# A byte limit on the loads under way in the first blocks of an attention and softplus-FFN kernel

## The chip, the cores and the metric

The kernel runs on one core of a Trainium2 chip. Its time is the device time of one execution in microseconds (us); of several executions the median is given. A core has five engines that run side by side, each with its own queue of instructions in a fixed order: PE (TensorE, matmuls), DVE (VectorE), ACT (ScalarE), POOL (GpSimd) and SP (SyncE, which here only issues transfers). The transfers themselves are carried out by 16 DMA engines. Engines wait for each other, and for transfers, on semaphores.

## The reference

The input is `q`, `k`, `v` of shape (4, 8, 768, 64) in float32 and two weight matrices in float64, `w_in` (512 x 2048) and `w_out` (2048 x 512). First comes a linear attention with a decay per head, then a feed-forward layer with softplus:

```python
for t in range(S):                      # S = 768
    state = gamma * state + outer(k[:, :, t], v[:, :, t])
    y[:, :, t] = scale * (q[:, :, t] @ state)
x = y.transpose(0, 2, 1, 3).reshape(3072, 512)
h = x @ w_in
g = maximum(h, 0) + log1p(exp(-abs(h)))
out = g @ w_out
```

## The kernel before

**Tiles.** The 3072 tokens are cut into 6 blocks of 512, and each block into 4 units of 128 tokens. A unit of attention loads its `q`, `k` and `v` (`qn`, `kn`, `vn`: 768 KB for all 8 heads; `q` and `k` as two transfers of 128 KB, `v` as one of 256 KB), scales `q` and `v` by the decay (POOL, L444 and L440), turns `q` and `k` on PE (L466, L474), copies them to `kt` (ACT, L481 and L482), and makes scores, states and outputs by 64x64 matmuls. Its result `x` is held as a high and a low part. The feed-forward layer goes over 16 slices `f` of 128 hidden columns: `hp = x @ w_in[:, f]`, softplus on DVE and ACT (L671 to L674, with the high part `gh` by ACT and the low part `gl` by POOL), and `acc += g @ w_out[f]`. All products are made of three matmuls, from high and low parts.

**Weights.** Each slice needs two loads of 512 KB of float64 words (`raw`): one of `w_in` (L362) and one of `w_out` (L364). They are taken apart on ACT and DVE (L369, L373, L379, L384, L389), and stored as a high part (ACT, L392) and a low part (POOL, L393). This is done once, in the first blocks of work, beside the attention and the matmuls that use the first slices.

**What sets the order.** A planner in the kernel collects all operations with a cost, a due time and their dependencies, plays them through with a clock of its own, and puts them out by planned start. Loads are operations of the engine SP with `size / rate` as cost (the helper `DMA`), so the order in which SP issues transfers is fixed at build time. The orders are tied down for every engine in `emit`.

**What SP waits for.** All transfers that matter here are issued by SP, one after the other; while one waits, all behind it wait. A load waits for the engines that last used its buffer. Beside that, landings are told by eight semaphores (DMAHW0 to DMAHW7) used in turn, each load taking the next one, so that a load waits for the landing of the one eight places before it.

**The first rows of SP.** In the order of SP, rows 1 to 13 load the attention units c00, c01 (half of the heads each) and c1; rows 14 and 15 load `w_in` of slices 0 and 1; rows 16 to 20 load the unit c2; rows 21 and 22 load `w_out` of slices 0 and 1; rows 23 to 27 load c3; rows 30 and 31 are `w_in` of slices 2 and 3, rows 32 and 35 `w_out` of slices 2 and 3. Rows 1 and 2 hold two loads each; every other row is one load. Rows 42, 46 and 48 are `w_in` of slices 4, 5 and 6, rows 45, 47 and 49 the `w_out` of these slices.

Of the kernel before, what the change touches and what calls it, by code (L numbers as in the profile page):

```python
# [30 lines left out]
PAIRED = 8  # L31
AFTER = 1000
FLIGHT = 3
VISITS = (1,3,6,9,11,14)
FILL = (8, 20, 15, 150)
EASY = 2
# [206 lines left out]
def decay_attention_then_softplus_ffn(ctx: ExitStack, tc: tile.TileContext, q, k, v, w_in, w_out, qtab, vtab, gtab, out):  # L243
# [14 lines left out]

    behind = mybir.DependencyInfo(mybir.DependencyClass.NoSync, mybir.DependencyReason.SCHED_ONLY)
    last = {}  # L260

    def emit(i):
        e = i.ins.engine
        if e in last:
            tc.add_manual_dep(i.ins, last[e], behind, reason="program order")
        last[e] = i.ins.name
        return i

    plan = Planner()
# [70 lines left out]
        return op  # L340

    def DMA(size, run, after=(), uses=(), at=None, rate=340.0):
        return plan.add("SP", size / rate, run, after, uses, at)

    mm = lambda o, l, r, start, stop: emit(nc.tensor.matmul(o, lhsT=l, rhs=r, start=start, stop=stop))  # L345


    wdone, pace = {}, []

    def convert_weights(f):  # L350
        n = ND * P
        fs = slice(f * P, (f + 1) * P)
        for nm in ("win", "wout"):
# [6 lines left out]
            def load(raw=raw, nm=nm):  # L360
                if nm == "win":
                    emit(nc.sync.dma_start(buf(raw).rearrange("p (c w) -> p c w", c=ND), w_in[:, fs].rearrange("(c p) w -> p c w", p=P)))  # L362
                else:
                    emit(nc.sync.dma_start(buf(raw), w_out[fs, :]))  # L364

            bits = lambda held: bank(held).bitcast(U32)
            free = [ys[u] for u in range(BORROW)] if f"{nm}{f}" in LATE else []
            ld = DMA(8 * P * n, load, free + [pace[-2 * FETCH]] if len(pace) >= 2 * FETCH else [], [raw])
            a = ACT(685, lambda word=word: emit(nc.scalar.activation(word(1).bitcast(F32), word(1).bitcast(F32), AF.Copy, scale=2.0**-112)), [ld], [raw])  # L369
            if nm == "wout" or f < EASY:  # L370
# [30 lines left out]
    def unit(p, first, G, when, paired):  # L401
# [27 lines left out]
        def fetch(size, run, held):  # L429
            loads.append(DMA(size, run, loads[-FLIGHT:-FLIGHT + 1] if paired else [], [held], when[0] - LOAD, 200.0))  # L430
            return loads[-1]
# [198 lines left out]
    def ffn_step(s, h, i, f, when, past_ops=()):  # L630
# [74 lines left out]
        for t in ts:  # L705
            acc, done = accs.pop((i, t))
            ob = hold_w(queue=False)
            if i == NB - 1:
                ob.among += ["win1", "win2"]
            if t % 2:  # L710
                o = ACT(scalar_time(DM), lambda acc=acc, ob=ob: emit(nc.scalar.copy(buf(ob), bank(acc))), [done[-1]], [acc, ob], when[1] + 3000)
            else:
                o = DVE(vector_time(DM), lambda acc=acc, ob=ob: emit(nc.vector.tensor_copy(buf(ob), bank(acc))), [done[-1]], [acc, ob], when[1] + 3000)
            r = slice(TURN[i * NT + t] * P, (TURN[i * NT + t] + 1) * P)
            DMA(4 * P * DM, lambda r=r, ob=ob: emit(nc.sync.dma_start(out[r, :], buf(ob))), [o], [ob], when[1] + 3000)
# [82 lines left out]
    for i, f in fs:  # L798
# [4 lines left out]
        if i < NB - 1:  # L803
# [3 lines left out]
            while m < min(target + EXTRA, NT * (i + 2), PAIRED):  # L807
                units((m, 0, 2, whens))
                m += 1
            if NT * (i + 1) >= PAIRED and f in VISITS:  # L810
                at = VISITS.index(f)
                if at % 3 == 0:
# [5 lines left out]
        ffn_step(None, None, i, f, (now - early * step, now + hidden_time + second_time + AFTER), past_ops)  # L818
        now += step + PACE

    ordered = plan.order()
    for op in ordered:
        op.run()


# [28 lines left out]
```

## Time and profile before

| | |
|---|---|
| runs | 755.79, 620.13, 622.18 us; median 622.18 us |
| profiled execution | 619.63 us, of which the span of instructions is 617.9 us |
| PE | 607.9 us busy, 98% of the span |
| PEld (weight loads) | 498.0 us, 81% |
| DVE, ACT, POOL | 241.2, 227.4, 239.9 us (37 to 39%) |
| data moved | 42.80 MB, mean 69 GB/s |
| granted TensorE clock | 1.0 throughout |

The span is what lies between the first and the last instruction; 1.7 us of the profiled execution lie outside it. Times in the trace count from the start of the span. "Idle before" is the time an engine stood still just before an instruction, with what ended the wait behind the arrow. A row of the list of DMA issues gives the kind, the number of loads, the size of one in KB and the microseconds from issue to landing; in a narrow window it is that of a single load.

### The profile page before, as it was taken

How to read it: one execution, taken by the hardware profiler on the slowest of the kernel's cores; microseconds unless marked ns; L12 is line 12 of the kernel's file. 1: busy time of each engine (PE TensorE's matmuls, PEld its weight loads, DVE VectorE, ACT ScalarE, POOL GpSimd, SP SyncE). 2: the span in 40 equal slices, each digit the busy share in tenths (PEclk: the TensorE clock that was granted, in tenths of full speed). 3: DMA queues.
4: the chain of work that ended last, by engine and by line, in shares of the span. 5: the costliest groups of instructions: out<-in, count | busy, mean ns of one | idle time of the engine just before them, and what ended most of it. 6: DMA issues, size and time to landing. Idle time of an engine off the chain costs nothing.

```text
span 617.9 us, 13254 instructions
## 1 busy us (share of the span) xinstructions
PE 607.9 (98%) x5635; PEld 498.0 (81%) x5635; DVE 241.2 (39%) x438; ACT 227.4 (37%) x407; POOL 239.9 (39%) x206
## 2 busy tenths in 40 slices
PE   8799999999999999999999999999999999999997
PEld 5688888888888878888888888888888888888886
DVE  4688776733323233322423332333323233322231
ACT  3768757641432234133134233143223313322221
POOL 3677768641342252153153143235225223222221
PEclk9999999999999999999999999999999999999999
DMA  7997566130120032040032031012103000100001
GB/s 187 267 282 221 187 210 184 57 103 2 35 54 16 2 86 86 1 87 17 3 86 86 1 82 25 1 45 76 53 2 86 1 1 1 69 1 1 1 0 68
DMA packets 90442, 42.80 MB, mean 69 GB/s; under 512 B 77072, under 2 KB 85264, under 8 KB 90384
## 3 DMA queue, kind: packets, MB, share of 16 engines
q1 hardware_dynamic: 89936, 41.95, 24.6%
q8 instruction: 44, 0.72, 0.5%
q14 instruction: 14, 0.11, 0.1%
q10 hardware_dynamic: 448, 0.01, 0.0%
HBM read 35.66 MB, written 6.29 MB: 68 GB/s over the span
## 4 chain that ended last, share of the span: by engine, by line
PE 95%; DMA 1%; SPq 1%; ACT 1%; DVE 1%; issue 0%; POOL 0%; ACTq 0%
PE hp L345 44%; PE acc L345 44%; PE a L345 4%; DMA raw<-in_moe_w_in_dram 1%; PE a L466 1%; PE a L474 1%; PE hp L466 1%; SPq L427 1%; DMA qn<-in_q_dram 0%; SPq L424 0%; DVE sp L673 0%; POOL win L393 0%; ACT gh L674 0%; ACT sp L672 0%; SPq L362 0%
## 5 line engine op out<-in xcount | busy, mean ns | idle before, releaser
L345 PE MATMUL hp<-x,win 128*128 128x512 f32 (+1 forms) x1176 | 278.0, 385 | 0.5 <-POOL win L393 0.5
L345 PEld LDWEIGHTS hp<-x,win 128*128 128x128 f32 x1176 | 217.4, 188 | 44.6 <-POOL win L393 0.7
L675 POOL TENSOR_TENSOR gl<-sp,gh 128x512 fp32r<-128x512 f32 x90 | 116.0, 1289 | 278.7 <-ACT gh L674 186.0
L345 PE MATMUL acc<-wout,gh 128*128 128x512 f32 x736 | 192.2, 396 | 0.5 <-DVE x L562 0.5
L345 PEld LDWEIGHTS acc<-wout,gh 128*128 128x128 f32 x736 | 134.9, 188 | 31.0 <-ACT gh L674 0.8
L671 DVE TENSOR_SCALAR sp<-hp 128x512 uint32<-128x512 uint32 x92 | 63.6, 691 | 243.5 <-PE hp L345 167.5
L672 ACT ACTIVATE sp<-sp 128x512 f32<-128x512 f32 x92 | 58.1, 632 | 261.1 <-DVE sp L671 261.0
L345 PE MATMUL acc<-wout,gl 128*128 128x512 f32 x368 | 104.8, 390 | 0.0
L673 DVE SCALAR_TENSOR_TENSOR sp<-hp,sp 128x512 f32<-128x512 f32 x92 | 63.5, 691 | 52.7 <-ACT sp L672 52.3
L345 PEld LDWEIGHTS acc<-wout,gl 128*128 128x128 f32 x368 | 69.0, 188 | 14.6
L674 ACT CAST gh<-sp 128x512 fp32r<-128x512 f32 x90 | 55.8, 620 | 60.0 <-DVE sp L673 59.9
L444 POOL TENSOR_TENSOR qn<-qn,tabs 128x512 f32<-128x512 f32 (+1 forms) x23 | 23.8, 1034 | 31.9 <-DMA qn<-in_q_dram 31.7
L596 POOL TENSOR_TENSOR x<-xs,x 128x512 fp32r<-128x512 f32 x20 | 25.6, 1295 | 12.6 <-ACT x L595 12.6
L440 POOL TENSOR_TENSOR vn<-vn,tabs 128x512 f32<-128x512 f32 (+1 forms) x24 | 24.2, 1010 | 8.2 <-DMA vn<-in_v_dram 8.0
L393 POOL TENSOR_TENSOR win<-w,win 128x512 fp32r<-128x512 f32 x16 | 20.6, 1293 | 8.5 <-ACT win L392 7.9
L369 ACT ACTIVATE raw<-raw 128x512 f32<-128x512 f32 x32 | 21.4, 676 | 6.8 <-DMA raw<-in_moe_w_in_dram 3.8
L393 POOL TENSOR_TENSOR wout<-w,wout 128x512 fp32r<-128x512 f32 x16 | 20.6, 1297 | 5.4 <-ACT wout L392 5.4
L384 DVE SCALAR_TENSOR_TENSOR a<-raw,a 128x512 uint32<-128x512 uint32 x28 | 19.2, 691 | 2.1 <-ACT a L373 1.7
L389 DVE SCALAR_TENSOR_TENSOR w<-raw,a 128x512 uint32<-128x512 uint32 x28 | 18.9, 683 | 1.6 <-POOL wout L393 0.5
L500 DVE TENSOR_TENSOR ah<-a,mask 128x256 uint32<-128x256 uint32 x27 | 10.3, 420 | 13.9 <-PE a L345 13.9
L592 DVE TENSOR_TENSOR xs<-a,xs 128x256 f32<-128x256 f32 (+1 forms) x24 | 8.8, 409 | 17.7 <-ACT xs L586 17.5
L595 ACT CAST x<-xs 128x512 fp32r<-128x512 f32 x20 | 12.4, 620 | 2.6 <-DVE xs L592 2.5
(138 smaller groups left out, 390.7 us busy)
## 6 DMA issues: line engine op xcount, KB each, us to landing
raw<-in_moe_w_in_dram SPq DMA_DIRECT2D x16, 512.0 KB, 6.3
raw<-in_moe_w_out_dram SPq DMA_DIRECT2D x16, 512.0 KB, 6.8
qn<-in_q_dram SPq DMA_DIRECT2D x44, 128.0 KB, 3.1
kn<-in_k_dram SPq DMA_DIRECT2D x44, 128.0 KB, 3.5
vn<-in_v_dram SPq DMA_DIRECT2D x22, 256.0 KB, 3.7
out_dram<-w SPq DMA_DIRECT2D x22, 256.0 KB, 2.2
out_dram<-win SPq DMA_DIRECT2D x2, 256.0 KB, 2.1
qn<-in_q_dram SPq DMA_DIRECT2D x4, 64.0 KB, 2.4
```

The source lines that it names most:

```text
L345: mm = lambda o, l, r, start, stop: emit(nc.tensor.matmul(o, lhsT=l, rhs=r, start=start, stop=stop))
L369: a = ACT(685, lambda word=word: emit(nc.scalar.activation(word(1).bitcast(F32), word(1).bitcast(F32), AF.Copy, scale=2.0**-112)), [ld], [ ...
L384: lambda word=word, wp=wp: emit(nc.vector.scalar_tensor_tensor(bits(wp), word(1), 0x80000000, bits(wp), op0=ALU.bitwise_and, op1=ALU.bitwi ...
L393: low_ = POOL(1300, lambda nm=nm, w=w: emit(nc.gpsimd.tensor_tensor(hl(nm, f)[:, 1], buf(w), hl(nm, f)[:, 0].bitcast(F32), op=ALU.subtract ...
L440: emit(engine.tensor_tensor(heads(held), heads(held), by, op=ALU.mult))
L444: emit(engine.tensor_tensor(all_, all_, by, op=ALU.mult))
L596: xl = POOL(2.53 * E * C, lambda: emit(nc.gpsimd.tensor_tensor(xo(1), buf(xs)[:, :E], xo(0).bitcast(F32), op=ALU.subtract)), [xh] + xdeps, ...
L671: a = DVE(vector_time(T), lambda: emit(nc.vector.tensor_scalar(U(spv()), U(bank(hp)), 0x80000000, None, op0=ALU.bitwise_or)), [lasts[-1]] ...
L672: b = ACT(640, lambda: emit(nc.scalar.activation(spv(), spv(), AF.Softplus)), [a], [sp])
L673: c = DVE(vector_time(T), lambda: emit(nc.vector.scalar_tensor_tensor(spv(), bank(hp), 0.0, spv(), op0=ALU.max, op1=ALU.add)), [b], [hp, sp])
L674: e = ACT(scalar_time(T, False), lambda: emit(nc.scalar.copy(buf(gh), spv())), [c], [sp, gh])
L675: g = POOL(1300, lambda: emit(nc.gpsimd.tensor_tensor(buf(gl), spv(), buf(gh).bitcast(F32), op=ALU.subtract)), [e], [sp, gh, gl])
```

## The change

Each SP operation now remembers its size. When the planned order is put out, each load adds up sizes backwards over the loads before it, beginning with its own. The load at which the sum passes 1,300,000 bytes is the one it must wait for: a wait on the landing of that load. Waits are added only where the planned start of the load lies before 60 us. The order on all engines is the same as before, row by row.

```diff
+UNDERWAY = 1.3e6
+SETTLED = 60000
...
     last = {}
+    issued = []
 
     def emit(i):
         e = i.ins.engine
         if e in last:
             tc.add_manual_dep(i.ins, last[e], behind, reason="program order")
         last[e] = i.ins.name
+        issued.append(i.ins)
         return i
...
     def DMA(size, run, after=(), uses=(), at=None, rate=340.0):
-        return plan.add("SP", size / rate, run, after, uses, at)
+        op = plan.add("SP", size / rate, run, after, uses, at)
+        op.size = size
+        return op
...
+    landed = mybir.DependencyInfo(mybir.DependencyClass.Sync, mybir.DependencyReason.DATA)
+    moved = []
     ordered = plan.order()
     for op in ordered:
         op.run()
+        if op.engine == "SP":
+            total = op.size
+            for size, instruction in reversed(moved):
+                total += size
+                if total > UNDERWAY:
+                    if op.start < SETTLED:
+                        tc.add_manual_dep(issued[-1], instruction.name, landed, reason="bytes under way")
+                    break
+            moved.append((op.size, issued[-1]))
```

What differs is what SP waits for. These are rows 14 to 22 of SP before (`raw` are weights, `qn`, `kn`, `vn` the inputs of unit c2):

```order
L362 DMA raw_190<-in_moe_w_in_dram 128x4x128 [waits DMAHW3_49]
L362 DMA raw_192<-in_moe_w_in_dram 128x4x128 [waits DMAHW4_49]
L427 DMA qn0_213<-in_q_dram 128x4x64 [waits DMAHW5_49,DVE_49,PE_49]
L427 DMA qn0_213<-in_q_dram 128x4x64 [waits DMAHW6_49]
L427 DMA kn0_230<-in_k_dram 128x4x64 [waits DMAHW7_49,DVE_49,PE_49]
L427 DMA kn0_230<-in_k_dram 128x4x64 [waits DMAHW0_49]
L424 DMA vn0_251<-in_v_dram 128x8x64 [waits DMAHW1_49,PE_49,Pool_49]
L364 DMA raw_260<-in_moe_w_out_dram 128x512 [waits DMAHW2_49]
L364 DMA raw_272<-in_moe_w_out_dram 128x512 [waits DMAHW3_49]
```

And the same rows now:

```order
L368 DMA raw_190<-in_moe_w_in_dram 128x4x128 [waits DMAHW6_49,DMAHW3_49]
L368 DMA raw_192<-in_moe_w_in_dram 128x4x128 [waits DMAHW4_49,DMAHW2_49]
L433 DMA qn0_213<-in_q_dram 128x4x64 [waits DMAHW5_49,DVE_49,PE_49]
L433 DMA qn0_213<-in_q_dram 128x4x64 [waits DMAHW3_49]
L433 DMA kn0_230<-in_k_dram 128x4x64 [waits DMAHW7_49,DVE_49,PE_49]
L433 DMA kn0_230<-in_k_dram 128x4x64 [waits DMAHW0_49]
L430 DMA vn0_251<-in_v_dram 128x8x64 [waits DMAHW1_49,DMAHW4_49,PE_49,Pool_49]
L370 DMA raw_260<-in_moe_w_out_dram 128x512 [waits DMAHW5_49]
L370 DMA raw_272<-in_moe_w_out_dram 128x512 [waits DMAHW1_49]
```

A row r uses the semaphore (r + 5) mod 8. Row 15 waited for row 7 (DMAHW4) and now also for the landing of row 13 (DMAHW2), the 256 KB of `v` just two places before it. Row 17 waits for row 14 (DMAHW3), row 20 for row 15 (DMAHW4), row 22 for row 20 (DMAHW1): two places back, where it was eight. Where a semaphore has gone from a row, an earlier row of SP already waits for the same landing or a later one.

Rows 30 to 35 before, two `w_in`, a `w_out`, two loads of `q`, a `w_out`:

```order
L362 DMA raw_403<-in_moe_w_in_dram 128x4x128 [waits DMAHW3_49]
L362 DMA raw_410<-in_moe_w_in_dram 128x4x128 [waits DMAHW4_49]
L364 DMA raw_488<-in_moe_w_out_dram 128x512 [waits DMAHW5_49]
L427 DMA qn1_507<-in_q_dram 128x4x64 [waits DMAHW6_49,PE_49,Pool_49]
L427 DMA qn1_507<-in_q_dram 128x4x64 [waits DMAHW7_49]
L364 DMA raw_519<-in_moe_w_out_dram 128x512 [waits DMAHW0_49]
```

And now:

```order
L368 DMA raw_403<-in_moe_w_in_dram 128x4x128 [waits DMAHW6_49]
L368 DMA raw_410<-in_moe_w_in_dram 128x4x128 [waits DMAHW4_49,DMAHW1_49]
L370 DMA raw_488<-in_moe_w_out_dram 128x512 [waits DMAHW5_49,DMAHW3_49]
L433 DMA qn1_507<-in_q_dram 128x4x64 [waits PE_49,Pool_49]
L433 DMA qn1_507<-in_q_dram 128x4x64 [waits DMAHW7_49,DMAHW4_49]
L370 DMA raw_519<-in_moe_w_out_dram 128x512 [waits DMAHW5_49,DMAHW0_49]
```

Row 32 now waits for row 30 (DMAHW3), and row 35 for row 32 (DMAHW5); row 35 had waited for row 27 (DMAHW0). The last row with an added wait is row 57, which waits for row 54.

## Prediction

> **What bounds the kernel now.** I read the page first, for who is busy when.
>
> ```profile
> PE 607.9 (98%) x5635; PEld 498.0 (81%) x5635; DVE 241.2 (39%) x438; ACT 227.4 (37%) x407; POOL 239.9 (39%) x206
> GB/s 187 267 282 221 187 210 184 57 103 2 35 54 16 2 86 86 1 87 17 3 86 86 1 82 25 1 45 76 53 2 86 1 1 1 69 1 1 1 0 68
> ```
>
> PE is busy 98% of the span, and the transfers are dense in the first seven of 40 slices alone (7 x 15.4 = 108 us). Next come the windows, split where PE's real matmuls begin and where it has no gaps any more.
>
> ```profile
> 0.00:20.40 20.40, 15.76 (x290) 10.78 (x291) 9.48 (x31) 8.50 (x20) 6.57 (x16) 1.00 0.80 193
> 20.40:41.00 20.60, 19.01 (x347) 16.16 (x345) 15.86 (x32) 15.29 (x30) 15.10 (x14) 1.00 1.03 270
> 41.00:617.90 576.90, 573.10 (x5003) 471.02 (x5001) 215.90 (x377) 203.65 (x360) 218.23 (x178) 1.00 0.21 58
> ```
>
> The number behind the length is PE's busy time, the last two are the share and the rate of the DMA engines. After 41 us PE works 573.1 of 576.9 us. So a PE delay at any point before that moves the end by as much, and the change can gain only from PE's gaps before 41 us. The chain of waits names the first gate, and PE's timeline the gaps:
>
> ```profile
> 9.48 7.25 DMA raw<-in_moe_w_in_dram
> 16.76 0.66 ACT raw L369
> ...
> 18.90 0.65 PE L474 MATMUL a<-ident,qn 128*128 128x128 f32 x4 [1.72 <-POOL qn L444]
> 21.37 1.45 PE L345 MATMUL hp<-x,win 128*128 128x256 f32 x10 [0.49 <-POOL win L393]
> 30.06 1.20 PE L345 MATMUL acc<-wout,gh 128*128 128x512 f32 x4 [0.47 <-DVE x L562]
> ```
>
> Row 15 of SP, the second `w_in`, is issued at 9.48 us and lands at 16.73; ACT begins on it at once. The three gaps of PE after that sum to 1.72 + 0.49 + 0.47 = 2.7 us.
>
> Then the landings. ACT's timeline gives those of the weights it stood waiting for, which are rows 14, 22, 30, 32, 35, 45 and 47 of SP:
>
> ```profile
> 15.19 0.67 ACT L369 ACTIVATE raw<-raw 128x512 f32<-128x512 f32 x1 [2.08 <-DMA raw<-in_moe_w_in_dram]
> 23.12 0.70 ACT L369 ACTIVATE raw<-raw 128x512 f32<-128x512 f32 x1 [0.17 <-DMA raw<-in_moe_w_out_dram]
> 30.02 0.68 ACT L369 ACTIVATE raw<-raw 128x512 f32<-128x512 f32 x1 [0.20 <-DMA raw<-in_moe_w_in_dram]
> 32.82 0.67 ACT L369 ACTIVATE raw<-raw 128x512 f32<-128x512 f32 x1 [0.67 <-DMA raw<-in_moe_w_out_dram]
> 36.51 0.67 ACT L369 ACTIVATE raw<-raw 128x512 f32<-128x512 f32 x1 [1.01 <-DMA raw<-in_moe_w_out_dram]
> 45.76 0.68 ACT L369 ACTIVATE raw<-raw 128x512 f32<-128x512 f32 x1 [0.31 <-DMA raw<-in_moe_w_out_dram]
> 48.49 0.66 ACT L369 ACTIVATE raw<-raw 128x512 f32<-128x512 f32 x1 [0.40 <-DMA raw<-in_moe_w_out_dram]
> ```
>
> For the others, issue by SP's timeline and flight by the list of issues in narrow windows (rows 13, 20 and 35, then the loads of 50.38, into an empty line, and of 52.21):
>
> ```profile
> 8.16 0.51 SPq L424 DMA_DIRECT2D win<-in_v_dram  x1
> 15.45 1.03 SPq L424 DMA_DIRECT2D vn<-in_v_dram  x1
> 28.50 0.62 SPq L364 DMA_DIRECT2D raw<-in_moe_w_out_dram  x1
> 50.38 1.24 SPq L427 DMA_DIRECT2D kn<-in_k_dram  x2
> 52.21 0.58 SPq L362 DMA_DIRECT2D raw<-in_moe_w_in_dram  x1
> ...
> win<-in_v_dram SPq DMA_DIRECT2D x1, 256.0 KB, 4.2
> vn<-in_v_dram SPq DMA_DIRECT2D x1, 256.0 KB, 4.6
> raw<-in_moe_w_out_dram SPq DMA_DIRECT2D x1, 512.0 KB, 8.0
> kn<-in_k_dram SPq DMA_DIRECT2D x1, 128.0 KB, 2.2
> raw<-in_moe_w_in_dram SPq DMA_DIRECT2D x1, 512.0 KB, 4.5
> ```
>
> So row 13 lands at 12.4 and row 20 at 20.0; all land in the order of issue. Rows 46 and 47 (512 KB each) take from 45.75 to 48.47, 1.4 us each: that is the pace of a full line, and row 35's 8.0 us are mostly time in the line. Into an empty line 128 KB land in 2.2 us, of which 1.4 / 4 = 0.35 is the data: the latency of a load is about 1.85 us.
>
> **What a wait can do.** SP's order is unchanged, and the line is served in that order, so holding a load back cannot bring an earlier one forward: it only shortens its stay in the line. The price is a bubble, if the line runs dry before the held load arrives. When a load is released, at most 1.3 MB less its own size are left under way. Behind 512 KB the line lasts 1.4 us, so a held load costs 1.85 - 1.4 = 0.45 us; behind 256 KB it costs 1.85 - 0.7 = 1.15 us; behind 640 KB 0.1.
>
> But the landing that counts is that of the slowest of 16 engines, and two rows show how far they part: the rate in 40 slices of 0 to 45 us (1.125 us each), and that of 48 to 52 us (0.1 us each).
>
> ```profile
> GB/s 0 49 115 150 159 124 184 227 200 254 269 309 333 238 191 139 202 314 353 322 260 214 222 205 336 342 361 337 313 338 275 153 64 205 234 317 326 267 371 384
> ...
> GB/s 451 420 328 410 440 471 307 266 430 266 184 113 62 41 41 82 41 0 41 41 164 41 0 41 41 0 0 0 0 0 0 0 0 0 82 115 159 210 259 241
> ```
>
> Up to 16.9 us the first 15 slices carry 2802 x 1.125 = 3.15 MB, but rows 1 to 15 are 2.62 MB: the 0.52 MB of rows 16 to 19 had nearly all moved before row 15 was told as landed. In the second row the line is nearly dry from 49.2 us on, and yet some 41 GB/s trickle until 50.5. So laggards of over a microsecond set the landings. A bubble on the other engines costs nothing until it exceeds that, and a laggard waits only where its own line is shorter than 1.85 us.
>
> **Place by place**, with the rows on which the cover rests:
>
> ```profile
> 26.26 0.59 ACT L482 COPY kt<-a 128x512 f32<-128x512 f32 x1 [1.08 <-PE a L474]
> 41.41 0.62 ACT L674 CAST gh<-sp 128x512 fp32r<-128x512 f32 x1
> 52.88 0.69 ACT L369 ACTIVATE raw<-raw 128x512 f32<-128x512 f32 x1
> 17.80 1.05 POOL L444 TENSOR_TENSOR qn<-qn,tabs 128x512 f32<-128x512 f32 x1 [4.28 <-DMA qn<-in_q_dram]
> 49.74 1.28 POOL L393 TENSOR_TENSOR win<-w,win 128x512 fp32r<-128x512 f32 x1 [0.79 <-ACT win L392]
> 42.59 2.11 PE L345 MATMUL acc<-wout,gh 128*128 128x512 f32 x8
> 52.21 0.85 PE L345 MATMUL hp<-x,win 128*128 128x512 f32 x3
> ```
>
> - Row 15 waits for row 13 (12.4) and is issued 2.9 us later; queued behind it on SP are the loads of unit c2. It needs 1.85 + 1.4 = 3.25 us, so it could land from 15.7, while row 14 holds the line until 15.2 and 1.4 more: 16.6, as now. Cost 0; with the 4.5 us of the load of 52.21 it lands at 16.9, so at most 0.2.
> - Row 17 waits for row 14 (15.2) and could land at 17.4; POOL began on it at 17.80. Cost 0, at most 0.6 if it flies 0.8 longer.
> - Row 22 waits for row 20 (20.0) and lands at 20.0 + 3.25 = 23.25 against 23.10: 0.15, covered by ACT's 1.08 us of idle time before 26.26.
> - Row 32 waits for row 30 (30.0): 33.25 against 32.8, +0.45. Its slice is multiplied at 48 us; it costs what it passes on to row 35.
> - Row 35 waits for row 32, with 256 KB behind that: plainly +0.45 + 1.15 = 1.6 at most. ACT takes it at 36.51, and then does copies, casts and a softplus in fixed order up to `gh` (41.41 + 0.62 = 42.03), which PE needs at 42.59: 0.56 us of cover. PE loses between 0 and 1.0. It lands at 36.5, while the rate is down to 153 and 64 GB/s from 34.9 on: a laggard sets it, and the others were done a microsecond earlier. I take 0.2, near the lower end.
> - Row 47 waits for row 45 (45.75): +0.45, and what row 35 passes on, so 0.45 to 2.0. Behind it on ACT stands the cast of `w_in` of slice 4, then POOL's low part, done at 51.02. PE's matmuls on it begin at 52.21, a cover of 1.2 us. PE loses 0 to 0.8; I take 0.2.
> - The later added waits, up to row 57, meet conversions that come well after the landing: ACT takes row 48 at 52.88, some three us after it lands. Cost 0, at most some tenths.
>
> The sum is 0.4 us, between 0 and 0.2 + 0.6 + 1.0 + 0.8 = 2.6. Against the profiled execution that is 619.6 + 0.4 = 620.0. The undisturbed runs, 620.1 and 622.2, lie 0.5 to 2.6 above the profiled one, in the middle 1.5, so I expect a median near 621.5.
>
> The Trainium skill speaks against the change: "DMA: Bandwidth & Descriptors", in its rules for kernel authors, asks to issue a transfer early and wait for it late, so that the fixed setup overlaps. By it each of the six waits above would expose its latency, 6 x 1.85 = 11 us and a median near 632; the trace shows the latency, but also a line behind which most of it vanishes.
>
> **The rivals.**
> - *Bubbles are not hidden (slower).* Every held 512 KB takes the 4.5 us of the load of 52.21, 1.25 more than reckoned. Rows 22, 32, 35 and 47 each land that much later on top of the upper sum: 4 x 1.25 + 2.6 = 7.6 us, less ACT's idle time there (1.08 + 1.01 + 0.40 = 2.5), so 5 us: 624.7, with the offset of 1.5 about 626. It decides from the point where row 35 lands after 37.1 us (36.5 + 0.56). For it: the rate falls to 64 GB/s at 36 to 37 us even now. Against: the 4.5 us hold the data of the loads just ahead.
> - *Less under way, shorter transfers (faster).* PE's gaps could close: at most 2.7 us, 616.9, with the offset 618.4. For it: a flight of 8 us against 2.2. Against: the rate is highest (371 and 384 GB/s at 43 to 45 us) where five loads of 512 KB stand in the line. The Trainium skill ("DMA: Bandwidth & Descriptors", latency and other measured facts) says that the access to HBM takes longer at high load and that a lighter load lowers the fixed cost; no row here separates that from the line.
> - *The waits are void.* The rule of eight loads already holds the others back, so that the awaited landing is always past. Then the time is that of before, 621.1 by the middle of the two runs. Row 15 speaks against: it was issued 2.9 us before row 13 landed.
>
> **How the numbers follow.** The forecast, a PE delay under 1.5 us, gets 0.60; slower by bubbles 0.17; faster 0.13; void waits 0.07; something the trace doesn't show 0.03. The likeliest time is 621.5. The range reaches from just below the faster rival, 618.0, to the bubbles' 626. A difference under 2% (12.4 us) is about what a measurement of this kernel can tell from no change. No case reaches it: PE's idle time before 41 us is 4.64 + 1.59 = 6.2 us in all, so faster by 2% gets 0.01; slower gets the 0.03 of the unseen; within 2% is 0.96.
>
> **What would show it.** In the profile after, row 15 issued near 12.4 and still landing at 16.6 to 16.9; flights of the later 512 KB loads of 3.3 to 4.5 us in place of 8; the wait of ACT at 36.5 moved by less than 1.6; PE without gaps from 42 us on. I am wrong if PE's matmuls on `w_in` begin before 20 us (a landing came forward), or if PE shows new gaps of over 1 us between 36 and 55 us.

## The result and the profile after

| | before | after |
|---|---|---|
| median | 621.24 us | 625.78 us (625.22 to 627.56, six executions) |
| ratio after / before | | 1.0088, 95% interval 1.0069 to 1.0106 |
| profiled execution | 619.63 us, span 617.9 | 627.56 us, span 625.8 |

The ratio leaves out one execution of before that took 755.79 us; the other five have a median of 620.31. The change costs 5.5 us (4.3 to 6.6, the ratio times 621). That is well under 2%, but clearly not zero: intervals of some 0.2% to either side tell far less than 2% from no change, against what the prediction says of that. I had forecast a loss of 0.4 us, in effect none. What came is near the rival "bubbles are not hidden", priced at 626. In what follows the microseconds of a kernel against before are its ratio of that kind, times 621.

The page of after, for the same lines as before:

```profile
PE 612.6 (98%) x5635; PEld 500.7 (80%) x5635; DVE 240.6 (38%) x438; ACT 227.4 (36%) x407; POOL 239.8 (38%) x206
...
PEclk9889999999999999999999999999999999999999
...
GB/s 148 223 210 238 294 157 107 180 35 85 1 86 17 2 86 85 1 85 18 2 69 98 5 42 46 18 6 80 86 1 86 1 1 1 68 1 1 1 0 67
```

The span grew by 7.9 us: PE is busy 4.7 us longer for the same 5635 matmuls, and idle for the other 3.2. Two stretches at half clock, in which PE was busy for 3.19 and 3.33 us (last section), explain some 3.3 us of the 4.7, by the estimate that a matmul takes twice as long there. The transfers are no longer done in seven slices; the eighth still carries 180 GB/s where it had 57. The windows of after (length, busy time of PE, PEld, DVE, ACT and POOL, then granted clock, DMA share and GB/s) put it in place:

```profile
0.00:20.40 20.40, 15.36 (x279) 10.32 (x280) 8.23 (x29) 7.95 (x18) 6.16 (x15) 0.98 0.73 175
20.40:41.00 20.60, 16.92 (x320) 13.50 (x319) 11.53 (x26) 11.85 (x23) 11.44 (x10) 0.91 0.75 208
41.00:60.00 19.00, 18.69 (x206) 15.17 (x204) 12.14 (x22) 11.17 (x21) 11.91 (x10) 0.93 0.85 223
```

From 20.4 to 41 us the rate is 208 GB/s where it was 270, and PE is busy for 16.92 us where it was 19.01. The chain of waits of after, its DMA links in order of time (start, us, what):

```profile
8.12 5.45 DMA win<-in_v_dram
14.06 3.90 DMA qn<-in_q_dram
17.98 5.81 DMA raw<-in_moe_w_out_dram
24.29 4.67 DMA kn<-in_k_dram
28.98 4.11 DMA raw<-in_moe_w_in_dram
33.10 5.18 DMA raw<-in_moe_w_out_dram
39.81 5.54 DMA vn<-in_v_dram
45.36 3.91 DMA raw<-in_moe_w_in_dram
49.33 4.00 DMA raw<-in_moe_w_out_dram
53.35 4.17 DMA raw<-in_moe_w_out_dram
```

Before, the chain had one such link after the start (9.48 to 16.73), and then went on through PE, POOL and DVE. Now it is loads end to end up to 57.5 us, one released by the landing of another. A held load of 512 KB flies 3.5 to 6.4 us from issue to landing (3.9 and 4.0 here at 45 and 49 us), where it stood up to 8.0 us in the line before; yet it lands later. The landings in us, as the trace has them:

| row | 15 | 20 | 32 | 35 | 47 |
|---|---|---|---|---|---|
| before | 16.73 | 20.02 | 32.79 | 36.49 | 48.47 |
| after | 17.39 | 22.49 | 38.28 | 42.14 | 57.52 |
| later by | 0.66 | 2.47 | 5.49 | 5.65 | 9.05 |

What that does to PE is in its timeline; these are its gaps of over 1 us after 16 us:

```profile
19.82 1.11 PE L480 MATMUL a<-ident,qn 128*128 128x128 f32 x4 [1.54 <-POOL qn L450]
28.59 0.66 PE L480 MATMUL a<-ident,qn 128*128 128x128 f32 x4 [1.22 <-POOL qn L450]
39.27 0.97 PE L351 MATMUL hp<-x,win 128*128 128x256 f32 x3 [1.53 <-ACT x L567]
```

The first two are the turning of `q` of c2 and c3, fed by loads of 128 KB, and not the weights. The third is the first at which a weight decides. ACT and DVE just ahead of it:

```profile
38.31 0.65 ACT L375 ACTIVATE raw<-raw 128x512 f32<-128x512 f32 x1 [1.72 <-DMA raw<-in_moe_w_out_dram]
...
38.87 0.35 ACT L567 CAST x<-a 128x256 fp32r<-128x256 f32 x1
39.12 0.38 ACT L567 CAST x<-acc 128x256 fp32r<-128x256 f32 x1
39.25 0.42 DVE L568 TENSOR_TENSOR x<-a,x 128x256 fp32r<-128x256 f32 x1 [3.37 <-ACT x L567]
```

ACT stands waiting for row 32, the third `w_out`, which in before PE multiplied only at 48 us, 15 us after its landing. Behind that wait, in ACT's fixed order, stand the casts of `x`, which PE needs at once.

The end is set later, and by gaps so small that they are easily passed over. The last load in the chain is row 47. ACT takes it at 57.54, and what stands behind it on ACT, DVE and POOL holds PE up twice:

```profile
60.15 0.50 PE L351 MATMUL hp<-x,win 128*128 128x512 f32 x1 [0.24 <-POOL win L399]
60.88 0.66 PE L480 MATMUL a<-ident,kn 128*128 128x128 f32 x4 [0.23 <-DVE xs L598]
```

In before the same matmuls, those behind the gap of 1.53 and those of 60.88, started here:

```profile
34.56 0.52 PE L345 MATMUL hp<-x,win 128*128 128x256 f32 x3
52.90 0.60 PE L474 MATMUL a<-ident,kn 128*128 128x128 f32 x4
```

So PE is 4.71 us late behind row 32, which landed 5.49 later, and 7.98 late behind row 47, which landed 9.05 later: covers of 0.8 and 1.1 us. After that the delay stays at 7.9 to 8.0 to the end. The kernels of the next section whose chain also ends its loads with row 47 bear it out: it landed 8.41, 8.34 and 5.99 us later than in before, and their spans grew by 7.3, 7.5 and 5.0 (no_35_45, after_filled, weights_held).

Why the loads land later is seen in the rate in 40 slices of 0.825 us from 16 to 49 us, first before, then after:

```profile
GB/s 214 91 259 158 344 338 366 300 265 196 228 229 189 293 359 336 359 358 325 300 370 297 251 162 63 146 183 217 295 344 315 239 373 361 372 391 375 369 386 370
```

```profile
GB/s 346 236 249 190 236 366 192 24 25 184 362 284 242 222 219 212 177 153 310 221 191 267 202 304 298 214 97 22 99 333 312 274 246 223 112 212 133 174 361 302
```

In after there are valleys of 22 to 25 GB/s, near 22.5 and near 38.5 us. The first looks like one engine at work: from 22.18 us to 23.43 the trace has nothing but eight packets of 4096 bytes, one behind the other, 155 ns apart, so 26 GB/s (and two of 4 bytes). Each load is split over the 16 engines, and its semaphore counts them one by one. These are the times in us at which the 16 counts came, for rows 20 and 21 of after:

```
row 20  20.20 20.27 20.31 20.33 20.36 20.38 20.38 20.45 20.55 20.57 20.58 20.60 20.69 20.90 20.98 22.49
row 21  21.55 21.59 21.61 21.64 21.66 21.72 21.81 21.83 21.84 21.86 21.90 21.92 21.95 22.14 22.25 23.79
```

15 of 16 engines had finished row 20 by 20.98 and row 21 by 22.25. Row 22 waits for row 20, was issued at 22.50 and landed at 26.03. So 15 engines had nothing to do for over a microsecond: row 22 was held back until the slowest one was done, and its data then took their time to come. The same holds at the first wait: row 13 was done on 15 engines at 11.98 and told as landed at 13.57. While it was under way one packet of 16 KB from the instruction queue ran from 11.01 to 11.97 us; that it held up that very engine is likely, but the trace does not name the engine. The fourteen traces of this case support it: of the loads of rows 13 to 47, 133 of the 334 that were under way while such a packet ran have a last count over 0.8 us behind the fifteenth, and 9 of the other 156.

### The profile page after: what moved, and what is told of

The parts are those of the page before. It is cut to its first block, busy times and chain, and to the rows that moved or that the text cites. A ratio compares the mean times of both kernels' runs of the same rounds, so it can differ in the third digit from the quotient of the medians.

```text
span 625.8 us, 13264 instructions
## 1 busy us (share of the span) xinstructions
PE 612.6 (98%) x5635; PEld 500.7 (80%) x5635; DVE 240.6 (38%) x438; ACT 227.4 (36%) x407; POOL 239.8 (38%) x206
## 4 chain that ended last, share of the span: by engine, by line
PE 89%; DMA 8%; SPq 1%; ACT 1%; DVE 0%; issue 0%; ACTq 0%
PE hp L351 42%; PE acc L351 42%; PE a L351 4%; DMA raw<-in_moe_w_out_dram 3%; DMA raw<-in_moe_w_in_dram 1%; DMA qn<-in_q_dram 1%; DMA vn<-in_v_dram 1%; DMA win<-in_v_dram 1%; SPq L433 1%; PE a L472 1%; DMA kn<-in_k_dram 1%; PE hp L472 1%; PE a L480 0%; DVE sp L679 0%; ACT sp L678 0%
## 5 line engine op out<-in xcount | busy, mean ns | idle before, releaser
L375 ACT ACTIVATE raw<-raw 128x512 f32<-128x512 f32 x32 | 21.5, 676 | 17.6 <-DMA raw<-in_moe_w_out_dram 9.5
L598 DVE TENSOR_TENSOR xs<-a,xs 128x256 f32<-128x256 f32 (+1 forms) x24 | 8.8, 408 | 17.6 <-ACT xs L592 17.5
L601 ACT CAST x<-xs 128x512 fp32r<-128x512 f32 x20 | 12.4, 620 | 2.4 <-DVE xs L598 2.2
```

## The experiments

**The dose.** Four kernels differ from after in the bound alone.

```diff
-UNDERWAY = 1.3e6
+UNDERWAY = 2.6e6     # limit_2600k; 1.9e6, 1.6e6 and 0.8e6 in the other three
```

> The limit is doubled to 2.6 million bytes; all else is as in the changed kernel. Theory of the dry line (a held load pays its latency because what is left under way runs out before it arrives): up to 2.1 MB stay under way, about 5.6 us of line at 1.4 us per 512 KB, so no bubble, and the time is that of before within 1 us (620 to 622 us). Theory of the clock (the loss comes from PE's half clock after gaps): no gaps of 1.5 us beyond the one of before, the same time. Theory of the wait itself (any wait on a landing in SP's queue costs, whatever its limit): 622 us or more.

> The limit is raised to 1.9 million bytes, one load of 512 KB more under way than with 1.3. Dry line: behind 1.05 to 1.3 MB the line lasts 2.8 to 3.5 us, against a latency of some 2.2 to 2.7 us (flights of 3.5 to 4.1 us less 1.4 us of data in the changed kernel), so most of the loss goes: 0.5 to 1.5 us over before. Wait itself: about as slow as with 1.3 million, 4 us over before or more.

> The bound raised from 1.3 to 1.6 MB. At a release up to 1.05 MB is then still under way, which the line carries in 1.05 / 512 KB x 1.4 = 2.9 us, and the new load's first bytes come after 2.1 to 2.6 us (flights of 3.5 to 4.0 measured for the held 512 KB loads of the changed kernel, less 1.4). If only an empty line cost time, by the mean of all 16 engines, nothing is left to lose: 0 to 0.5 us over the kernel before. If the wait on the slowest of the 16 engines eats the rest of the line (the engines' landings lie 1.5 to 2 us apart in the kernel before), the other engines still run dry: 1.5 to 3 us over before. 1.9 MB cost nothing and 1.3 MB cost 4.5 to 5.5.

> The limit is lowered to 0.8 million bytes: a load of 512 KB goes out when at most 256 KB are left under way. Dry line: the rate is what is under way over the flight. With about 0.7 MB per 4 us, some 170 GB/s, the 8.65 MB of rows 16 to 47 take about 50 us, 10 us more than the 40 us of the changed kernel; PE loses most of that: 633 to 640 us. Wait itself (a fixed price per wait, as many waits as before): 626 to 628.

| bound | median us | ratio to before | rows 15 to 47, from landing to landing |
|---|---|---|---|
| none (before) | 620.5 to 621.4 | 1 | 31.7 us |
| 2.6 MB | 620.93 | 1.0010 (0.9993 to 1.0027) | 34.2 us |
| 1.9 MB | 620.59 | 1.0002 (0.9991 to 1.0012) | 31.6 us |
| 1.6 MB | 620.60 | 0.9994 (0.9973 to 1.0016) | 34.0 us |
| 1.3 MB (after) | 625.78 | 1.0088 (1.0069 to 1.0106) | 40.1 us |
| 0.8 MB | 647.15 | 1.0409 (1.0368 to 1.0450) | 52.7 us |

The windows of one stretch, 16.7 to 48.5 us, in before, in the kernels with 1.6 MB, with 1.3 MB (after), and with 0.8 MB:

```profile
16.70:48.50 31.80, 28.49 (x463) 23.80 (x455) 24.48 (x48) 22.69 (x43) 22.68 (x20) 1.00 1.03 285
```

```profile
16.70:48.50 31.80, 29.47 (x497) 24.04 (x493) 23.50 (x47) 21.94 (x41) 21.88 (x19) 1.00 0.96 255
```

```profile
16.70:48.50 31.80, 26.48 (x437) 21.73 (x441) 19.30 (x37) 19.00 (x36) 18.09 (x16) 0.89 0.85 217
```

```profile
16.70:48.50 31.80, 19.58 (x365) 15.91 (x365) 12.52 (x26) 11.71 (x23) 11.41 (x10) 0.84 0.62 164
```

So the price is not that of a wait as such: with 1.9 MB under way the line is as fast as without waits. What counts is how much the bound leaves under way: 285, 255, 217, 164 GB/s. The first two may differ by chance alone, since 1.9 MB has 270 and 2.6 MB 260; the last two do not. Between 1.3 and 1.6 MB lies the point at which time is lost. Whether the line itself loses anything at 1.6 MB is open: its 34.0 us are 2.3 more than in before, but 2.6 MB has 34.2 and the kernel that holds row 35 alone 34.5, at times within 1 us of before. These are single executions, and 31.6 to 34.5 us is what a line that is hardly held takes. By the prediction's price 1.6 MB leaves no bubble (768 KB or more remain at a release, 2.1 us of line against 1.85 of latency). With 0.8 MB the time was above what had been expected (633 to 640), though the rate was as expected: PE waits 3.35, 3.56 and 5.06 us at the same three places, and 1.64 and 2.24 more at 67.35 and 73.92 us.

```profile
22.06 1.12 PE L480 MATMUL a<-ident,qn 128*128 128x128 f32 x4 [3.35 <-POOL qn L450]
34.68 1.06 PE L480 MATMUL a<-ident,qn 128*128 128x128 f32 x4 [3.56 <-POOL qn L450]
49.34 1.25 PE L351 MATMUL hp<-x,win 128*128 128x256 f32 x3 [5.06 <-ACT x L567]
```

**The stage.** Only the waits of rows 14 to 27, and only those of rows 28 to 57:

```diff
-SETTLED = 60000
+SETTLED = 18000                          # waits_early
...
-                    if op.start < SETTLED:
+                    if 18000 < op.start < SETTLED:   # waits_late
```

> The limit of 1.3 million bytes holds for rows 14 to 27 of SP only (planned start before 18 us). Dry line: what the changed kernel had lost by 33 us, 2 to 3 us over before, since PE has no gaps later in which it could be regained. Rival, a single place: the loss comes from row 32 alone, behind which ACT holds the copies of x; then this run is within 0.5 us of before. Clock: one stretch of half clock at 19.6 to 23 us stays, at most 1.7 us of the loss.

> The limit holds for rows 28 to 57 only (planned start from 18 to 60 us). Dry line: the rest of the loss, 4 to 5 us over before, adding up with the run for the early rows to the 4.5 to 8 us of the changed kernel. A single place (row 32): 4 us over before or more, nearly all of the loss, with the early rows costing nothing.

Early: 622.97 us, 1.0048 (1.0033 to 1.0063), so 3.0 us. Late: 623.76 us, 1.0060 (1.0045 to 1.0075), so 3.7 us. Each half costs, and together (6.7) they make about the whole of 5.5 (4.3 to 6.6). The largest gaps are those of after: the turning of `q` of c2 in the first kernel, the casts of `x` behind row 32 in the second.

```profile
20.73 1.12 PE L480 MATMUL a<-ident,qn 128*128 128x128 f32 x4 [2.89 <-POOL qn L450]
```

```profile
36.81 0.96 PE L351 MATMUL hp<-x,win 128*128 128x256 f32 x3 [1.30 <-ACT x L567]
```

So the early rows, whose cost the prediction took as 0 (at most 0.8), carry nearly half of the loss. Not all of it is the wait: in the first kernel's trace PE is 1.83 us late at 20.73, and the delay grows to 3.49 at 26.03 without a gap, in a stretch at half clock (19.05 to 25.88); 3.0 remain to the end.

**The kind of load.** Waits on the loads of weights alone, and on those of attention alone:

```diff
-                    if op.start < SETTLED:
+                    if op.start < SETTLED and op.size > 5e5:   # weights_held
+                    if op.start < SETTLED and op.size < 5e5:   # attention_held
```

> The limit of 1.3 million bytes holds for the 512 KB loads of weights only; loads of q, k and v go out without it. Dry line: what counts are the loads that come behind a short line, which are those of 512 KB: 4 us over before or more (624.5 to 626). Rival, the attention loads are what is late (PE's gaps at 19.8 and 28.6 us ended with the scaling of q): most of the loss goes, 622 or less.

> The other half: the limit holds for the loads of q, k and v only, the weights go out without it. Dry line: a held load of 128 KB stands behind one or two full loads of 512 KB, so it costs little: 0 to 1 us over before (620.5 to 621.7). Attention loads late: 623 or more.

Weights: 625.22 us, 1.0070 (1.0045 to 1.0095), 4.3 us. Attention: 622.79 us, 1.0033 (1.0015 to 1.0051), 2.0 us where 0 to 1 had been expected. The second shows that a held small load costs as well: PE waits for POOL on `q` of c3.

```profile
28.72 1.11 PE L480 MATMUL a<-ident,qn 128*128 128x128 f32 x4 [2.84 <-POOL qn L450]
```

**Single waits.** Row 35 alone, the place where the prediction put its largest term; then all waits but those of rows 35 and 45, the two that leave only 256 KB in the line:

```diff
-                    if op.start < SETTLED:
+                    if len(moved) == 36:                                   # only_row_35
+                    if op.start < SETTLED and len(moved) not in (36, 46):  # no_35_45
```

> Only row 35 (a block of w_out) waits, on the landing of row 32; the other added waits are gone. The prediction's term for row 35 alone was a bubble of up to 1.6 us with a loss of 0.2 us on TensorE, 0 to 1.0. If the bubble is as measured in the changed kernel (1.6 us) and the later loads keep nothing of it, 0.2 again, not to be told from no change. If a loss on the line is never won back while the loads are behind, all that exceeds the 0.56 us of cover is lost: about 1.0 us over before.

> The changed kernel without the waits of rows 35 and 45, the two that leave only 256 KB in the line at their release (reckoned bubble 1.85 - 0.7 = 1.15 us each; measured in the changed kernel 1.6 and 1.5 us). All other added waits stay: by the reckoned prices, added up over all held rows 15 to 47, they keep 6.15 - 2.3 = 3.85 of 6.15 us of bubbles; by the landings (8.4 us later in all between rows 15 and 47) 8.4 - 3.1 = 5.3. If bubbles add up along the line, the time falls by 2 to 3 us against the changed kernel: 622 to 624, 1.5 to 3 over before. If the loss were that of rows 35 and 45 alone, 0 to 0.5 over before. If each wait costs what its own place has no cover for, whatever the others do, rows 35 and 45 alone would be worth at most what the time of the waits of rows 28 on showed, 3.1 us.

Row 35 alone: 621.66 us, 1.0002 (0.9985 to 1.0019), so between a gain of 0.9 and a loss of 1.2 us; that does not part 0.2 from 1.0. In its trace the row was issued at 34.79, right after row 32 had landed, and landed at 38.46, a flight of 3.67 us. From row 34's landing to its own are 3.02 us, against 2.71 in before: the bubble is there, but before had almost the same hole at this place. PE has no gap over 0.3 us between 20 and 47 us.

Without rows 35 and 45: 626.31 us, 1.0072 (1.0047 to 1.0097), 4.5 us. I had expected 1.5 to 3; a loss of up to 3 is just within the interval, but the trace speaks against it: row 35 lands at 41.65 and row 47 at 56.88, where after has 42.14 and 57.52. Setting two loads free brought them forward by 0.5 and 0.6 us. The reason is the row ahead: row 34, a load of `q` that waits for row 31, was issued at 37.10, and row 35 comes behind it in SP's queue. Row 31 itself came late through one engine; its 16 counts, and what ACT and PE made of it:

```
row 31  34.12 34.13 34.15 34.16 34.31 34.36 34.40 34.45 34.46 34.47 34.51 34.65 34.66 34.95 35.42 37.09
```

```profile
37.11 0.65 ACT L375 ACTIVATE raw<-raw 128x512 f32<-128x512 f32 x1 [3.29 <-DMA raw<-in_moe_w_in_dram]
38.43 0.65 ACT L375 ACTIVATE raw<-raw 128x512 f32<-128x512 f32 x1 [0.67 <-DMA raw<-in_moe_w_out_dram]
```

```profile
39.40 0.96 PE L351 MATMUL hp<-x,win 128*128 128x256 f32 x3 [1.71 <-ACT x L567]
```

So the gate is row 32 again, at 38.41 us and with about the same gap on PE as in after (1.71 against 1.53), and row 47 after it. The loss can't be told off wait by wait: take some of the waits away, and the others hold the line to the same bytes.

**The clock.** The granted clock of after falls to half in two stretches (the last section shows them). To see whether that is the loss, after was given extra matmuls on data already there, ahead of the three places where PE waits; the same was done to before at the first place.

```diff
+                            for _ in range(13):        # after_filled: ahead of the first hp of the second half of tokens
+                                emit(nc.tensor.matmul(spare[:, :W], lhsT=word[:, :P], rhs=word[:, :W], start=True, stop=True))
...
-            rest = PE(..., lambda n=n: emit(nc.tensor.matmul(bank(idles)[:, :n], ...)), ...)
+            rest = PE(..., lambda n=n, i=i: [emit(nc.tensor.matmul(bank(idles)[:, :n], ...)) for _ in range({35: 13, 42: 10}.get(i, 1))], ...)
                                                        # before_filled: {35: 13}
```

> The changed kernel with 13, 10 and 13 dummy matmuls of some 0.11 us each (bf16, 128x256, the result never read) in front of the three places where PE stood still for 1.2 to 1.5 us in its profile (transposes of c2 and c3, first matmuls of x on w_in for the second half of tokens). The clock's share of the loss: if stretches of half clock after the gaps cost what they last (3.4 us at half speed, 1.7 us each, one or two per run), the granted clock goes to 0.999 or more and the time falls by 1.5 to 3.4 us, to 622.5 to 624. If PE waits for loads in those stretches anyway, the clock rises and the time stays at 625 to 626. Dry line alone: no change of the landings, a time of 624 to 626.

> The kernel before with 13 extra matmuls (on data that is there, results unused) ahead of the transposes of c2, where TensorE otherwise waits near 20 us. Leaves nothing out. In executions of before that show one stretch of 3.41 us at half clock (mean clock 0.997) the time is about 1 us above those that show none. If the wait ahead of that stretch is what brings the clock down, the executions with it go, and the median falls by 0 to 0.3 us, none at 0.997; if not, the median is unchanged or up to 0.5 us above.

After with fillers: 626.90 us, 1.0090 (1.0061 to 1.0120), no better than after. Two of its four executions ran at a mean clock of 1.0, at 626.46 and 626.69 us; the other two, at 0.996 and 0.997, were 627.1 and 628.6. Before with fillers: 622.46 us, 1.0020 (0.9999 to 1.0041), and six of twelve executions still show a clock of 0.996 or 0.997, so the wait at c2 is not what brings the clock down in those. But its other six, at 0.999 or 1.0, have a median of 622.0, where the 18 such executions of before have 620.4: the fillers at one place cost up to 1.6 us themselves, and three places may have eaten what the clock gave back. What parts the two is kernels without fillers. weights_held has one execution at a clock of 1.0, with 625.09 us, and waits_late three at 0.999 or 1.0, with 622.94 to 624.16; before at 0.999 or 1.0 beside them has medians of 620.4 and 620.1. So a loss of 3 to 5 us is there at full clock. In the trace of after the delay of PE does grow from 4.7 to 6.9 us without a gap between 39.27 and 43.55, most of it at half clock, but by the landings PE would have had to wait as long for row 47; that is argued, not tested. In waits_early no such wait came later, and there the half clock is part of the 3.0 us.

No version tried beats before; 1.6 to 2.6 MB can't be told from it.

## Why the prediction was wrong

- **The failed step is how late the loads become: the price of the bubbles, and the sum made of them.** I priced six waits, each against its own cover, and let each start from the landings of before ("Row 22 waits for row 20 (20.0)", "Row 32 waits for row 30 (30.0)", "Row 47 waits for row 45 (45.75)"). But in after 17 releases between rows 15 and 47 hung on an added wait, and a hole in the line is not won back while the loads are behind: every landing after it is later. With the prediction's own prices, seven waits behind 512 KB (0.45 each), eight behind 640 KB (0.1) and two behind 256 KB (1.15) make 3.15 + 0.8 + 2.3 = 6.25 us (the expectation for the kernel without rows 35 and 45 has 6.15). The line lost 40.1 - 31.7 = 8.4, or 5.6 against the 34.5 of the slowest line that is hardly held. The eleven waits that I left out hold 3.2 of the 6.25, row 45 with 1.15 above all, which stands in the same position as row 35.
- **Row 47** is where the sum should have been set: "+0.45, and what row 35 passes on, so 0.45 to 2.0", against a cover of 1.2. The cover was right (1.1 in after), but the landing was 9.05 us later. The prediction's own prices, summed and set against that one cover, give 6.25 - 1.2 = 5 us; 5.5 were measured.
- **"A bubble on the other engines costs nothing until it exceeds that" had it the wrong way round.** I read from the 41 GB/s at the end of before's line that single engines lag by over a microsecond, and concluded that bubbles on the others cost nothing. In before no load is released by the landing of one two or three places ahead, and the other engines go on with the next loads. In after the release itself waits for the laggard (row 20: 20.98 for 15 engines, 22.49 for the last), so its delay is handed to all 16; five of the 17 releases came over a microsecond after the fifteenth count. How much of the 8.4 us is due to that stays open: 2.15 lie beyond the prices, but lines differ by nearly 3 us between executions, and no run took the laggards away. The Trainium skill ("DMA: Bandwidth & Descriptors", "Why a DMA increments its semaphore by 16 and not by 1") says that only the full count means that all data has landed; the releases here fit that, each after the sixteenth count.
- **Row 15**, "issued near 12.4 and still landing at 16.6 to 16.9": issued at 13.59 and landed at 17.39, because row 13 was told as landed 1.2 us later than before. That is more likely chance than the change: with bounds of 1.6 to 2.6 MB row 13 landed at 13.4 to 14.0 too. Its own flight, 3.8 us, lies in the range I gave. Cost taken 0 (at most 0.2), and it was 0.66 on the landing.
- **Row 17**, "Cost 0, at most 0.6": issued at 15.01, not at 15.2, but it flew 3.55 us, landed at 18.56 (17.64 in before), and PE turned `q` of c2 at 19.82 in place of 18.90, so 0.92. Of rows 16 to 21 no other has a term in the sum. Row 20 landed 2.47 us later, and the waits of rows 14 to 27 alone cost 3.0 us (2.0 to 3.9). One reservation: in the kernel that holds only row 35, row 20 landed at 21.56 too, without any wait there, so single landings vary by 1.5 us between executions, and the time over many executions counts more than one landing.
- **Row 32**, "its slice is multiplied at 48 us; it costs what it passes on to row 35": wrong. I looked for the user of the data, and not for what stands behind the wait on ACT. The casts of `x` do, in before's timeline of ACT too, directly behind the 32.82 that the prediction quotes. Row 32's cover, 0.8 us, was the one to reckon there, not row 35's.

```profile
33.38 0.36 ACT L561 CAST x<-a 128x256 fp32r<-128x256 f32 x1
33.63 0.39 ACT L561 CAST x<-acc 128x256 fp32r<-128x256 f32 x1
```

- **Row 35**, a bubble of 1.6 us at most with 0.2 on PE: alone, the step was not refuted. That a laggard sets the landing there in before held (2.71 us between landings against 3.02). In after it lands 5.65 us later, where I had said less than 1.6, but nearly all of that it inherits.
- **The latency** of 1.85 us came from a lone load of 128 KB. Flights of held loads of 512 KB were 3.5 to 4.2 us at seven of eleven places (up to 6.4 at the others), less 1.4 of data, so 2.1 to 2.8: the latency was taken too small by 0.25 to 0.95. They lie between the 3.25 that I took and the rival's 4.5.
- **My sign for being wrong**, "new gaps of over 1 us between 36 and 55 us", came at 39.27 with 1.53. "PE without gaps from 42 us on" held up to the two of 0.24 and 0.23 us at 60, which are those behind row 47. No landing of `w_in` came forward by more than 0.2 us.
- **The rival that won** said 626 through four loads that take 4.5 us each, deciding from the point where row 35 lands after 37.1. Row 35 landed at 42.14, and the time was 625.8. The size agrees, the path only partly: the loss is spread over most of the held rows, and enters PE at c2's and c3's `q`, at row 32 and at row 47, not at row 35. I gave it 0.17, and the argument against it ("the 4.5 us hold the data of the loads just ahead") held for part of the difference only, by those flights.
- **The Trainium skill's rule that the prediction sets against the change** (issue early, wait late) pointed the right way; 11 us was twice what came, since most of each latency does lie beside data under way.
- The rival "less under way, shorter transfers" got its shorter flights and lost by them: w_in and w_out take 4.6 and 5.6 us now from issue to landing, and ACT's wait for them rose to 17.6 us, from 6.8 in before.

```profile
L375 ACT ACTIVATE raw<-raw 128x512 f32<-128x512 f32 x32 | 21.5, 676 | 17.6 <-DMA raw<-in_moe_w_out_dram 9.5
...
raw<-in_moe_w_in_dram SPq DMA_DIRECT2D x16, 512.0 KB, 4.6
raw<-in_moe_w_out_dram SPq DMA_DIRECT2D x16, 512.0 KB, 5.6
```

## What to carry to other kernels

Add up the holes that all added waits make in a line, since in a line that is behind they sum, and set that sum against the cover behind the last of the held loads; look there for what stands behind the waiting instruction in its queue, not for who uses the data. Small gaps can be the ones that set the end: follow the chain, or compare the same instruction's start in both traces. A wait on a landing is a wait on the slowest engine: a bound on what is under way must leave enough for latency and for that spread, which here was more than 1.3 MB at some 280 GB/s, and 1.6 MB sufficed. In this kernel a line in which loads pile up was no fault, since the landings come in the order of issue, which is fixed.

## What the hardware showed beside that

**A window half idle halves the clock.** The granted clock changes in steps of 3.41 us. The windows of after, cut at these steps (PE's busy time is the first after the length, the clock the third from the end):

```profile
16.20:19.61 3.41, 1.48 (x50) 1.03 (x50) 1.93 (x5) 1.75 (x5) 0.89 (x1) 1.00 1.08 244
19.61:23.02 3.41, 3.19 (x15) 2.82 (x16) 1.90 (x5) 2.21 (x4) 1.81 (x3) 0.50 0.54 183
23.02:26.43 3.41, 3.41 (x84) 3.21 (x83) 1.27 (x2) 1.59 (x3) 1.92 (x2) 1.00 0.84 236
36.68:40.09 3.41, 1.81 (x8) 1.03 (x6) 0.84 (x2) 1.56 (x4) 0.79 (x1) 1.00 0.52 113
40.09:43.50 3.41, 3.33 (x17) 3.18 (x16) 3.19 (x6) 2.21 (x5) 1.54 (x2) 0.50 1.14 287
43.50:46.90 3.40, 3.40 (x24) 3.04 (x23) 2.53 (x4) 2.51 (x5) 2.72 (x3) 1.00 0.82 161
```

A window in which PE was busy for 1.48 or 1.81 us was followed by one at half clock, and a busy one brought full clock back. In before the gap of 1.72 us ahead of 18.90 fell into two windows, and the clock stayed; so it did after a window with 1.94 us of work in the kernel with the bound of 1.9 MB.

```profile
14.35:17.76 3.41, 2.20 (x58) 1.43 (x55) 1.78 (x4) 2.19 (x4) 0.00 (x0) 1.00 0.85 194
17.76:21.18 3.42, 1.98 (x16) 1.71 (x16) 2.88 (x6) 2.57 (x7) 2.19 (x2) 1.00 1.02 283
```

In the profiled executions of all fourteen kernels, cut at these steps, of the windows at full clock eleven with 0 to 1.49 us of PE work were all followed by half clock, and one with 1.81; with 1.93 us or more none was, and the kernel with 0.8 MB kept its clock after two of 1.77 and 1.79. So the limit lies at about half a window. The way back takes more: windows at half clock with 1.73, 2.16 and 2.52 us of work were followed by another, those with 3.09 or more by full clock. Where the windows begin differs from execution to execution, so the same gap halves the clock in one and not in another. The Trainium skill ("TensorE: Matmul & The Clock Gate", "What's actually happening" and "Why this matters for your kernels") has a free-running window of 3413 ns, with which the steps agree, but counts on an idle window and warns only of gaps above some 3 us; here half a window sufficed, with single gaps of 1.5 us. What it costs depends on what PE would wait for next: by the argument above nothing to speak of in after, and part of the 3.0 us in waits_early.

**Waits can draw the engines together.** After some held loads the 16 counts come within 0.5 to 0.6 us (rows 15 to 19 of after; row 15: 16.82 to 17.39), where they lay 1.7 to 2.6 us apart in before (row 15: 14.15 to 16.73). It does not hold everywhere: rows 20, 21 and 46 of after have spreads of 2.2 to 2.5 us. My reading is that after a dry line all start anew at the same time, and that the spread in before is work done ahead, not work lost; no run tests it.
